# First unit of attention: v sent from its own tile to the tiles the products read, asked for one step later

## The chip, the cores and the metric

The kernel runs on one core of one Trainium2 chip. The metric is the device time of one execution in microseconds (us); of several runs the median counts. The engines of the core work side by side, each through its own instructions in order: TensorE (PE, with its weight loads PEld), VectorE (DVE), ScalarE (ACT), GpSimd (POOL), and SyncE (SP), whose queue here issues every transfer between the core's on-chip memory and DRAM.

## What is computed

The input x has 2048 rows of 512. Six rows of modulation come from a small vector c. The kernel computes attention with 32 heads of width 16 and then a mixer with two further products and an MLP; the change lies in the attention alone:

```python
h = _layernorm(x, axis=-1) * (1 + ca) + sa
qkv = (h @ wqkv).reshape(B, S, 3, H, Dh).transpose(2, 0, 3, 1, 4)
q, k, v = qkv[0], qkv[1], qkv[2]
scores = jnp.einsum("bhqd,bhkd->bhqk", q, k) * (Dh ** -0.5)
p = _softmax(scores, axis=-1)
o = jnp.einsum("bhqk,bhkd->bhqd", p, v)
x = x + ga * (o.transpose(0, 2, 1, 3).reshape(B, S, D) @ wo)
h = _layernorm(x, axis=-1) * (1 + cb) + sb
x = x + gb * _B_ref(h, B_w1, B_w2, B_w3, B_w4)
```

## The kernel before

**Units and steps.** Attention is cut into 64 units: 4 chunks of 512 queries times 16 pairs of heads. A unit has 16 steps, one for each tile of 128 keys (kt 0 to 15), so there are 1024 steps s. In a step PE makes two score products (sc, L1001) and two score products of the step 24 ahead (mb, L985). DVE takes the maxima of the mb products (mx, L981), ACT the exponentials of the sc products (pt, L997), POOL the low half of the split probabilities (pt<-pt, L1049). Two blocks of three half steps later PE multiplies them by v (pv: L1075 for the high parts, four matmuls a step; L1072 for the low parts, four every two steps). The pv products of key tiles 4i to 4i+3 read v from the tile vst[i].

**Filler.** Between these blocks PE works off other products: those that make q, k and v (L338, L340, L342), those of the modulation rows (mr, L632), and later the mixer. A planner written into the kernel (class Sched) lays the order down when the program is built: it keeps a clock of its own for each engine and a credit for filler, and gives each block so much of it as the budget (800, 900, then 700 of its ns a step) allows. Where the attention needs something, drain or step pushes the generators on until the planner's flag is there, whatever the credit says.

**v.** The generator v_gen with v_tiles makes v in 16 tiles of 128 keys for 8 pairs of heads at once: twelve matmuls into one bank, then ACT (L752, L753), DVE (L738), ACT (L755) and POOL (L756) write the split parts into one of three rotating tiles vt. The function store, last in that chain, issues one transfer of 384 KB from vt to Vs in DRAM (Vs<-vt), in rows of 384 bytes. A tile vt can be written again by ACT when this transfer has read it. The attention reads Vs back by pair, four key tiles at a time (vst<-Vs, 192 KB, function load_v). For all units but the first these loads are issued by pv_part well ahead. For unit 0 the function before(s) does it: the table VAT names the steps before which the four groups are demanded, here -1, 1, 5 and 9; it drains until the planner takes the four stores of the group as landed, and then issues one load.

**Order on SP.** All transfers stand in one queue in the order in which the planner made them, and an instruction that waits there holds up those behind it. Between the v stores stand the rows of k and q for DRAM (Ks<-qk, Qs<-qk), the loads of the next units (qtl<-Qs, kst<-Ks), eight small writes of shifts for each unit (qtl<-nm), and the weights (wst).

Of the kernel before, what the change touches and what calls it, by code (L numbers as in the profile page):

```python
# [61 lines left out]
XL = 0  # L62
NQ = 6
NV = 3
VAT = (-1, 1, 5, 9)
NPT = 8
PLOAD = 3500.0
WLAT = 4000.0
# [228 lines left out]
def cA(n=CH):  # L297
    return n / 1.2 + 52


def cD(n=CH):
    return n / 0.96 + 69
# [7 lines left out]
def kernel(ctx, tc, A_x, A_wqkv, A_wo, B_w1, B_w2, B_w3, B_w4, c, w_mod, out):  # L310
    nc = tc.nc
    te, act, dve, pool, dma = nc.tensor, nc.scalar, nc.vector, nc.gpsimd, nc.sync
# [24 lines left out]
    def mm3(o, lh, ll, rh, rl, first, last):  # L337
        te.matmul(o, lh, rh, start=first, stop=False)  # L338
        yield
        te.matmul(o, lh, rl, start=False, stop=False)  # L340
        yield
        te.matmul(o, ll, rh, start=False, stop=last)  # L342
        yield

    def nsq(n):
        return 0.4405 * n + 6
# [9 lines left out]
    def v_hi(t):  # L356
        return t[:, :, 0:128].rearrange("p a (b n) -> p a b n", b=2)
# [20 lines left out]
    Vs = dr.tile([NP, P, NKT, 192], BF16, name="Vs")  # L378
# [13 lines left out]
    sch = Sched()  # L392
    done = set()
    psd = {"s": False}

    def dbank(n):
        return sch.take(lambda i: psd["d"].tile([P, CH], F32, name=n, tag=("v" if i == NSM else f"s{i}") if psd["s"] else f"d{i}", bufs=1))
# [58 lines left out]
    def halves(w, nk):  # L456

        return [w[:, i].rearrange("p (k n) -> p k n", k=nk) for i in range(2)]
# [256 lines left out]
        done.add(("v", a))  # L715

    vlive, vrs = [], [0]

    def v_tiles(w, a, kts):
        wh, wl = halves(w, KT)  # L720
        for kt in kts:
            ci, t = divmod(kt, TPC)
            h = hT[ci]
            yield lambda: len(vlive) < NV and vrs[0] < 2 and sch.room() and ("hT", ci) in done
            vrs[0] += 1
            vlive.append(kt)
            b = dbank("v")[:, :256]
            for k in range(KT):
                for _ in mm3(b, h[:, k, 0, t * P:(t + 1) * P], h[:, k, 1, t * P:(t + 1) * P],
                             wh[:, k], wl[:, k], k == 0, k == KT - 1):  # L730
                    yield nsq(256)
            w = vt[kt % NV]
            v, vl = v_hi(w), v_lo(w)
            b3 = b.rearrange("p (a b d) -> p a b d", b=2, d=DH)
            r = qp.tile([P, H // 4, 2, DH], F32, name="vr", tag="vr", bufs=2)

            def rest(v=v, b3=b3, r=r, b=b):
                dve.tensor_tensor(r, b3, v[:, :, :, 0:DH], op=OP.subtract)  # L738
                sch.free(b)

            def store(kt=kt, w=w):
                vrs[0] -= 1

                def gone():
                    vlive.remove(kt)
                    if kt % 4 == 3:
                        done.add(("v", a, kt // 4))
                e = sch.dma(dma.dma_start, Vs[8 * a:8 * a + 8, :, kt, :].rearrange("a p n -> p a n"),
                            w)
                sch.after(e, gone)  # L750

            sch.chain(("A", cA(256), lambda v=v, b3=b3: act.activation(v[:, :, :, 0:DH], b3, AF.Copy)),  # L752
                      ("A", cA(256), lambda vl=vl, b3=b3: act.activation(vl[:, :, :, 8:8 + DH], b3, AF.Copy, scale=1.0 / VHI)),  # L753
                      ("D", cD(256), rest),
                      ("A", cA(256), lambda v=v, r=r: act.activation(v[:, :, :, VD:VD + DH], r, AF.Copy)),  # L755
                      ("G", cG(256), lambda v=v, r=r: pool.tensor_tensor(v[:, :, :, 2 * VD:2 * VD + DH], r, v[:, :, :, VD:VD + DH],  # L756
                                                                         op=OP.subtract)),
                      (None, 0, store), prio=VP, bank=b)
# [130 lines left out]
    def drain(flag):  # L889
        while flag not in done:  # L890
            sch.step()
# [45 lines left out]
    unit_tiles(at, 1, pool, pool)  # L937
    qst, mxs, osb = {}, {}, {}
    vst = [at.tile([P, NKT // 4, 192], BF16, name=f"vst{i}") for i in range(4)]
    pv, pt = {}, {}  # L940
    pts = [at.tile([P, 2, CH], I32, name=f"pt{i}") for i in range(NPT)]

# [11 lines left out]
    def load_v(u, i):  # L954

        if (u, i) in vnext or not u:
            vnext.discard((u, i))
            if u:
                drain(("v", units[u][1] // 8, i))
            sch.dma(dma.dma_start, vst[i], Vs[units[u][1], :, 4 * i:4 * i + 4])  # L960
# [585 lines left out]
    def before(s):  # L1546

        if s > NS // NC and s % (NS // NC) == 16:
            drain(("oT", s // (NS // NC) - 1))
        nu, r = divmod(s + 32, 16)  # L1550
        if r == 0 and 0 < nu < NU:
            ci, pr = units[nu]
            drain(("kq", pr // 4))
            if ci:
                drain(("q", pr // 8))
            load_unit(nu)
        if s in VAT:
            drain(("v", 0, VAT.index(s)))
            load_v(0, VAT.index(s))
        if s == NS - 12:  # L1560
            done.add("keys")
        if s == -12:
            unit_tiles(at, 2, dve, pool)
# [109 lines left out]
```

## Time and profile before

| | us |
|---|---|
| median of 3 runs | 2008.15 (2007.61 to 2010.73) |
| the profiled execution | 2010.86 |
| its span | 2009.1 |
| PE busy in the span | 1920.7 (96%) |
| POOL busy | 1678.7 (84%) |
| DVE busy | 1652.4 (82%) |
| ACT busy | 1467.5 (73%) |

The profiled execution took 2010.86 us, of which the span of the records is 2009.1. Start of unit 0 (its first sc product) is at 97.66 us of the span. The profile puts every wait down to what came last, by engine and line; the time an engine sat idle stands in brackets with it. A row of the timeline has the start, the time until the last of a merged group ended, the engine and line, the names (out<-in) and the count. The granted clock of TensorE is given as a share of its 2.4 GHz.

### The profile page before, as it was taken

Reading aid. Unit: us, or ns where it says so; the run is one execution under the profiler, and the core shown is the slowest. Engines: PE = TensorE matmul, PEld = TensorE weight load, DVE = VectorE, ACT = ScalarE, POOL = GpSimd, SP = SyncE. Lnnn points to the kernel's source line nnn. Section 1 sums busy time; section 2 is a strip of 40 time slices with the busy share of each in tenths; the row PEclk is TensorE's granted clock in tenths of the full one; section 3 lists DMA queues with packets and bytes.
Section 4 is the critical chain, followed back from the end, with each engine's and each line's share of the span. In section 5 each row is a group of like instructions: output and inputs, shape, how many; then the busy total and the mean of one; then the engine's idle time right before and its main releaser. Section 6 shows DMA issues by size and latency. Waiting matters only on the chain.

```text
span 2009.1 us, 42336 instructions
## 1 busy us (share of the span) xinstructions
PE 1920.7 (96%) x14464; PEld 1143.8 (57%) x14464; DVE 1652.4 (82%) x3025; ACT 1467.5 (73%) x3074; POOL 1678.7 (84%) x1611
## 2 busy tenths in 40 slices
PE   6899999999899999999999999999999999999899
PEld 4655554555454555555455555555545555555798
DVE  8878888788998988888989888898898889892643
ACT  5365889778878887777878777787787778786443
POOL 5376999899999998888999998898898989897532
PEclk8999999999999999999999999999999999999999
DMA  5764777876553334344433333344433343333432
GB/s 187 203 193 148 209 226 229 263 233 200 190 172 110 114 111 149 94 136 160 125 114 98 108 108 112 110 135 136 152 102 98 112 134 116 110 116 111 182 143 90
DMA packets 230624, 293.24 MB, mean 146 GB/s; under 512 B 123636, under 2 KB 175348, under 8 KB 214120
## 3 DMA queue, kind: packets, MB, share of 16 engines
q1 hardware_dynamic: 230408, 290.53, 46.2%
q8 instruction: 115, 1.88, 0.4%
q14 instruction: 101, 0.83, 0.1%
HBM read 226.49 MB, written 62.91 MB: 144 GB/s over the span
## 4 chain that ended last, share of the span: by engine, by line
PE 65%; DVE 17%; ACT 8%; POOL 3%; issue 3%; DMA 2%; SPq 1%; POOLq 0%; ACTq 0%; DVEq 0%
PE mb L985 13%; DVE mx L981 10%; PE sc L1001 10%; PE pv L1075 10%; PE w L338 7%; PE w L342 6%; PE w L340 6%; PE pv L1072 4%; ACT pt L997 4%; POOL pt L1049 2%; PE mr L632 1%; DVE xs L1400 1%; DVE sq L1397 1%; ACT pt L126 1%; PE ot L1104 1%
## 5 line engine op out<-in xcount | busy, mean ns | idle before, releaser
L1049 POOL TENSOR_SCALAR pt<-pt 128x1024 f16<-128x1024 uint16 x992 | 1317.2, 1364 | 129.2 <-ACT pt L997 123.8
L981 DVE TENSOR_REDUCE mx<-mb 128x1 f32<-128x512 f32 x2048 | 1278.7, 680 | 77.5 <-PE mb L985 52.0
L997 ACT ACTIVATE pt<-sc 128x512 int32<-128x512 f32 x2048 | 1088.3, 608 | 273.9 <-PE mb L985 212.0
L985 PE MATMUL mb<-kst,qtl 64*128 64x512 f32 x2048 | 750.5, 453 | 46.8 <-ACT pt L997 14.3
L1001 PE MATMUL sc<-qtl,kst 64*128 64x512 f32 x2048 | 720.1, 445 | 5.2 <-DVE mx L981 1.9
L985 PEld LDWEIGHTS mb<-kst,qtl 64*128 64x128 f32 x2048 | 347.9, 193 | 248.7 <-DVE mx L981 90.1
L1001 PEld LDWEIGHTS sc<-qtl,kst 64*128 64x128 f32 x2048 | 337.1, 186 | 160.3 <-DVE mx L981 53.4
L1075 PE MATMUL pv<-pt,vst 128*32 128x512 f16 x4096 | 359.8, 398 | 3.5 <-DMA vst<-Vs 3.5
L1072 PE MATMUL pv<-pt,vst 128*25 128x512 f16 (+1 forms) x2048 | 211.7, 395 | 2.0 <-POOL pt L1049 1.9
L1075 PEld LDWEIGHTS <-vst 128*32 128x32 bf16 x4096 | 91.2, 95 | 170.6 <-issue 109.5
L338 PE MATMUL w<-A,wr 128*128 128x256 f32 (+2 forms) x576 | 175.6, 305 | 1.0 <-ACT A L332 0.6
L1407 POOL TENSOR_TENSOR g<-xs,g 128x256 fp32r<-128x256 f32 (+2 forms) x144 | 102.9, 716 | 86.9 <-ACT g L1406 84.7
L340 PE MATMUL w<-A,wr 128*128 128x256 f32 (+2 forms) x576 | 170.1, 295 | 0.7 <-DVE A L328 0.7
L342 PE MATMUL w<-A,wr 128*128 128x256 f32 (+2 forms) x576 | 167.5, 291 | 0.0
L338 PEld LDWEIGHTS w<-A,wr 128*128 128x128 f32 x576 | 109.7, 190 | 36.1 <-ACT pt L997 13.2
L338 PE MATMUL w<-wr,g 128*128 128x512 f32 x288 | 119.3, 414 | 0.6 <-ACT g L1406 0.6
L340 PEld LDWEIGHTS w<-A,wr 128*128 128x128 f32 x576 | 109.9, 191 | 13.2 <-issue 12.0
L342 PE MATMUL w<-wr,g 128*128 128x512 f32 x288 | 115.0, 399 | 0.7 <-POOL g L1407 0.7
L1514 DVE TENSOR_TENSOR x<-x,w 128x512 f32<-128x512 f32 x64 | 43.9, 686 | 85.5 <-PE w L342 85.4
L340 PE MATMUL w<-wr,g 128*128 128x512 f32 x288 | 113.7, 395 | 0.0
L342 PEld LDWEIGHTS w<-A,wr 128*128 128x128 f32 x576 | 110.0, 191 | 5.6 <-issue 5.6
L1403 ACT ACTIVATE sq<-w 128x256 f32<-128x256 f32 (+2 forms) x144 | 55.8, 387 | 72.3 <-PE w L342 69.6
(147 smaller groups left out, 2079.5 us busy)
## 6 DMA issues: line engine op xcount, KB each, us to landing
wr<-Ws SPq DMA_DIRECT2D x80, 1024.0 KB
vst<-Vs SPq DMA_DIRECT2D x256, 192.0 KB
kst<-Ks SPq DMA_DIRECT2D x189, 256.0 KB
qtl<-Qs SPq DMA_DIRECT2D x192, 64.0 KB
Vs<-vt SPq DMA_DIRECT2D x32, 384.0 KB
Ws<-wq SPq DMA_DIRECT2D x40, 256.0 KB
Ws<-wst SPq DMA_DIRECT2D x40, 256.0 KB
wst<-in_B_w_dram SPq DMA_DIRECT2D x36, 256.0 KB
```

What stands on the lines that cost most here:

```text
L338: te.matmul(o, lh, rh, start=first, stop=False)
L340: te.matmul(o, lh, rl, start=False, stop=False)
L342: te.matmul(o, ll, rh, start=False, stop=last)
L981: end = sch.crit("D", 605, e + PX, lambda: dve.reduce_max(mxs[u][:, j, g, c:c + 1], b, axis=AX.X))
L985: return ready, lambda: te.matmul(b, lhs, kst[u % 3][r, c * CH:(c + 1) * CH], start=True, stop=True), after
L997: ea = sch.crit("A", 480, e + PX, lambda: act.activation(pt[s][:, j], b, AF.Exp))
L1001: return ready, lambda: te.matmul(b, kst[u % 3][r, kt * P:(kt + 1) * P], qst[u][r], start=True, stop=True), after
L1049: e_low[s] = XP["G"] + sch.crit("G", 1345, ready, lambda: pool.tensor_scalar(o, i, 0.5, 1.0, op0=OP.mult, op1=OP.mult))
L1072: te.matmul(acc[r:r + n, :], v[:, (kt + i) % 4, c - n:c].bitcast(F16), pt[s + i].bitcast(F16)[:, j, 0::2], start=False, stop=kt == NKT - 2 ...
L1075: te.matmul(acc[r:r + 32, :], v[:, kt % 4, r:r + 32], pt[s].bitcast(F16)[:, j, 1::2], start=kt == 0, stop=False, skip_group_check=True)
L1403: sch.chain(("A", cA(n), lambda: act.activation(sq, b, AF.Square)), ("D", cD(n), cube), ("A", cA(n), lambda: act.activation(sq, sq, AF.Tan ...
L1407: ("G", cG(n), lambda: pool.tensor_tensor(lo, xs, hi, op=OP.subtract)), (None, 0, end), bank=b)
```

## The change

Unit 0 no longer reads its v back from DRAM where that can be avoided. For each tile of the first v pass (a = 0) that is stored after the attention's tiles exist, store issues one more transfer, ahead of the one to Vs: the part of pair 0, 128 rows of 384 bytes, from vt straight into its place in vst. That holds for key tiles 2 to 15, fourteen transfers of 48 KB. Key tiles 0 and 1 were stored before and are loaded from Vs one at a time (2 transfers of 48 KB). The four loads of 192 KB fall away. The demands move from steps -1, 1, 5, 9 to -1, 2, 6, 10, and what they wait for is now, in the planner, that store has been issued, not that it has landed.

```diff
-VAT = (-1, 1, 5, 9)
+VAT = (-1, 2, 6, 10)
...
+    direct, near = [], set()
...
             def store(kt=kt, w=w):
                 vrs[0] -= 1
 
+                if not a and direct:
+                    sch.dma(dma.dma_start, direct[kt // 4][:, kt % 4], w[:, 0])
+                    near.add(kt)
+
                 def gone():
                     vlive.remove(kt)
+                    done.add(("vk", a, kt))
                     if kt % 4 == 3:
                         done.add(("v", a, kt // 4))
...
     vst = [at.tile([P, NKT // 4, 192], BF16, name=f"vst{i}") for i in range(4)]
+    direct += vst
...
         if s in VAT:
-            drain(("v", 0, VAT.index(s)))
-            load_v(0, VAT.index(s))
+            i = VAT.index(s)
+            for kt in range(4 * i, 4 * i + 4):
+                while kt not in near and ("vk", 0, kt) not in done:
+                    sch.step()
+                if kt not in near:
+                    sch.dma(dma.dma_start, vst[i][:, kt % 4], Vs[0, :, kt])
```

Because the planner sees other drains and other times on SP, it lays the filler down otherwise. On PE the order differs between the first v products beside attention and step 231; before it and from step 232 on, the matmuls stand in the same order in both. Up to step 0 and up to step 9 as much filler has been done in both. From there 24 matmuls of k that stood between steps 24 and 30 come later, so that from step 30 on the filler is behind by up to 29 matmuls' worth of 512 columns (26 at step 30, 21 at step 40, 19 at step 104); the arrears are made up between steps 112 and 136, and after a small lead both are level at step 232.

SP, from the load or copy that fills vst for key tile 12 on; vst_607 is the tile vst[3], vst_604 is vst[0], which here is filled for unit 1. The kernel before:

```order
L105 DMA qtl_600<-nm 1x128x2 x8
L105 DMA vst_604<-Vs 128x768
L105 DMA Vs<-vt_172 128x8x192
L105 DMA Vs<-vt_164 128x8x192
L105 DMA Qs<-qk_158 128x2x512
L105 DMA Qs<-qk_159 128x512
L105 DMA wst_118<-in_A_wqkv_dram 128x2x128 x2
L105 DMA wst_114<-in_A_wqkv_dram 128x2x128 x2
L105 DMA vst_607<-Vs 128x768
```

The changed kernel:

```order
L105 DMA vst_607<-vt_164 128x192
L105 DMA Vs<-vt_164 128x8x192
L105 DMA qtl_600<-nm 1x128x2 x8
L105 DMA vst_604<-Vs 128x768
L105 DMA vst_607<-vt_168 128x192
L105 DMA Vs<-vt_168 128x8x192
L105 DMA vst_607<-vt_172 128x192
L105 DMA Vs<-vt_172 128x8x192
L105 DMA Qs<-qk_158 128x2x512
L105 DMA Qs<-qk_159 128x512
L105 DMA vst_607<-vt_164 128x192
L105 DMA Vs<-vt_164 128x8x192
```

The one load of vst[3], which stood behind the last stores, the q rows and four weight loads, is replaced by four copies, the first of them ahead of the eight small writes; key tile 13 is stored behind those writes instead of ahead of them, and key tile 15 behind the q rows.

POOL at the same place (pt_615 is the low half of step 7, nm the shifts of a unit). The kernel before:

```order
L756 TENSOR_TENSOR vt_168<-vr,vt_168 128x8x2x16
L1034 TENSOR_TENSOR nm<-mf,nm 128x8
L756 TENSOR_TENSOR vt_172<-vr,vt_172 128x8x2x16
L756 TENSOR_TENSOR vt_164<-vr,vt_164 128x8x2x16
L1049 TENSOR_SCALAR pt_615<-pt_615 128x1024
L1049 TENSOR_SCALAR pt_608<-pt_608 128x1024
```

The changed kernel:

```order
L762 TENSOR_TENSOR vt_164<-vr,vt_164 128x8x2x16
L1041 TENSOR_TENSOR nm<-mf,nm 128x8
L762 TENSOR_TENSOR vt_168<-vr,vt_168 128x8x2x16
L762 TENSOR_TENSOR vt_172<-vr,vt_172 128x8x2x16
L762 TENSOR_TENSOR vt_164<-vr,vt_164 128x8x2x16
L1056 TENSOR_SCALAR pt_615<-pt_615 128x1024
L1056 TENSOR_SCALAR pt_608<-pt_608 128x1024
```

Three tiles of v instead of two stand directly ahead of the low half of step 7; behind them 18 low halves follow in a row, where it were 16.

ACT some steps later (wp is a split of weights that waits for a weight load). The kernel before:

```order
L997 ACTIVATE pt_614<-sc 128x512 x2
L440 ACTIVATE wp<-wst_118 128x512
L997 ACTIVATE pt_615<-sc 128x512 x2
L440 ACTIVATE wp<-wst_114 128x512
L997 ACTIVATE pt_608<-sc 128x512 x2
L997 ACTIVATE pt_609<-sc 128x512 x2
L997 ACTIVATE pt_610<-sc 128x512 x2
L1093 ACTIVATE ac<-pv 128x512
```

The changed kernel:

```order
L1004 ACTIVATE pt_610<-sc 128x512 x2
L1100 ACTIVATE ac<-pv 128x512
L1004 ACTIVATE pt_611<-sc 128x512 x2
L1004 ACTIVATE pt_612<-sc 128x512 x2
L1004 ACTIVATE pt_613<-sc 128x512 x2
L1004 ACTIVATE pt_614<-sc 128x512 x2
L1004 ACTIVATE pt_615<-sc 128x512 x2
L1004 ACTIVATE pt_608<-sc 128x512 x2
L440 ACTIVATE wp<-wst_114 128x512
L440 ACTIVATE wp<-wst_115 128x512
```

The two weight splits, which stood among the last exponentials of unit 0, now come six steps into unit 1's products, behind the copy ac of unit 0's result.

## Rows read from the trace of the kernel before

**Rows 1.** The page: span, busy time of each engine, granted clock in 40 slices.

```profile
span 2009.1 us, 42336 instructions
PE 1920.7 (96%) x14464; PEld 1143.8 (57%) x14464; DVE 1652.4 (82%) x3025; ACT 1467.5 (73%) x3074; POOL 1678.7 (84%) x1611
PEclk8999999999999999999999999999999999999999
```

**Rows 2.** Waits from 60 to 200 us: total, times, longest.

```profile
POOL pt L1049 <- ACT pt L997: 25.9, 21, 4.5
...
PE pv L1075 <- DMA vst<-Vs: 3.5, 1, 3.5
```

**Rows 3.** Timeline of PE around that wait.

```profile
128.33 0.40 PE L1072 MATMUL pv<-pt,vst 128*17 128x512 f16 x4
132.25 0.62 PE L1075 MATMUL pv<-pt,vst 128*32 128x512 f16 x4 [3.52 <-DMA vst<-Vs]
```

**Rows 4.** Engines by stretch: busy us (count), then PEclk, DMA share, GB/s.

```profile
120.00:128.60 8.60, 8.38 (x76) 3.66 (x72) 8.29 (x14) 6.48 (x13) 8.60 (x7) 1.00 0.79 213
132.30:139.00 6.70, 6.70 (x38) 3.90 (x42) 5.08 (x8) 3.29 (x7) 3.47 (x3) 0.52 0.76 222
316.00:345.00 29.00, 27.94 (x207) 14.58 (x205) 24.51 (x43) 26.96 (x58) 28.84 (x27) 1.00 0.75 225
```

**Rows 5.** Timeline of SP, 110 to 130 us.

```profile
114.53 0.36 SPq L105 DMA_DIRECT2D Vs<-vt  x1
116.08 5.22 SPq L105 DMA_DIRECT2D qtl<-nm  x8
121.35 0.59 SPq L105 DMA_DIRECT2D vst<-Vs  x1
122.04 1.00 SPq L105 DMA_DIRECT2D Vs<-vt  x2
123.14 2.21 SPq L105 DMA_DIRECT2D Qs<-qk  x2
125.39 3.48 SPq L105 DMA_DIRECT2D wst<-in_A_wqkv_dram  x4
128.97 0.41 SPq L105 DMA_DIRECT2D vst<-Vs  x1
```

**Rows 6.** Timeline of POOL, 119 to 150 us.

```profile
119.82 10.34 POOL L1049 TENSOR_SCALAR pt<-pt 128x1024 f16<-128x1024 uint16 x8
132.08 1.34 POOL L1049 TENSOR_SCALAR pt<-pt 128x1024 f16<-128x1024 uint16 x1 [1.91 <-ACT pt L997]
134.92 1.33 POOL L1049 TENSOR_SCALAR pt<-pt 128x1024 f16<-128x1024 uint16 x1 [1.50 <-ACT pt L997]
137.99 2.65 POOL L1049 TENSOR_SCALAR pt<-pt 128x1024 f16<-128x1024 uint16 x2 [1.73 <-ACT pt L997]
141.40 5.21 POOL L1049 TENSOR_SCALAR pt<-pt 128x1024 f16<-128x1024 uint16 x4 [0.76 <-ACT pt L997]
146.89 2.69 POOL L1049 TENSOR_SCALAR pt<-pt 128x1024 f16<-128x1024 uint16 x2
```

**Rows 7.** Timeline of ACT: the last tile of v, and the weight split.

```profile
117.47 0.36 ACT L752 ACTIVATE vt<-v 128x256 bf16<-128x256 f32 x1
118.66 0.42 ACT L755 ACTIVATE vt<-vr 128x256 bf16<-128x256 f32 x1 [0.55 <-DVE vr L738]
...
130.32 0.63 ACT L440 ACTIVATE wp<-wst 128x512 fp32r<-128x512 f32 x1 [2.45 <-DMA wst<-in_A_wqkv_dram]
```

**Rows 8.** A store's landing: its issue on SP, and ACT's wait for it.

```profile
66.66 3.52 SPq L105 DMA_DIRECT2D Vs<-vt  x3
...
71.09 0.39 ACT L752 ACTIVATE vt<-v 128x256 bf16<-128x256 f32 x1 [1.56 <-DMA Vs<-vt]
```

**Rows 9.** Waits of SP from 60 to 130 us.

```profile
SPq L105 <- POOL vt L756: 11.1, 6, 3.5
SPq L105 <- DMA Vs<-vt: 2.6, 1, 2.6
```

**Rows 10.** PE: products of filler in a row (k of 512 columns, v of 256).

```profile
105.30 0.40 PE L340 MATMUL k<-hT,wp 128*128 128x512 f32 x1
105.53 0.39 PE L342 MATMUL k<-hT,wp 128*128 128x512 f32 x1
...
116.45 0.28 PE L340 MATMUL v<-wp,hT 128*128 128x256 f32 x1
116.57 0.28 PE L342 MATMUL v<-wp,hT 128*128 128x256 f32 x1
```

## The prediction

> **What bounds the kernel now.** I read the page first. PE is busy for 1920.7 of 2009.1 us and its granted clock is almost everywhere full [rows 1], so over the whole span PE sets the time, with POOL, DVE and ACT behind it. But the change reaches only unit 0 and, by the planner, the filler up to step 231; what follows has the same matmul order. So I read that stretch alone. The waits of the stretch show one in which PE waits for a transfer: 3.5 us, once, for vst<-Vs [rows 2]. The timeline of PE places it at 128.7 to 132.25 us, before a product of the high parts [rows 3]. The timeline of SP says why. The load that releases it is issued at 128.97 and lands at 132.25, 3.3 us later; it was issued so late because it stands behind the last two stores of v, two transfers of q and four weight loads, and waited 2.6 us for the last store to land [rows 5, 9]. The load brings all of key tiles 12 to 15, and PE wanted tile 12, which had been ready for long.
>
> A second row belongs to it. From 132.3 to 139.0 us the granted clock is 0.52 of full, that is almost throughout at the lower level of 1.2 GHz, directly behind the wait, and PE is busy all through [rows 4]. Third, the stretch around it has hardly any filler. There the engines of the softmax decide: POOL is busy 8.60 of 8.60 us up to the wait, and then 3.47 of 6.70 [rows 4]. Its timeline has eight low halves in 10.34 us, 1.30 each, then gaps of 1.91, 1.50, 1.73 and 0.76 us behind ACT [rows 6]. In that stretch ACT also waits 2.45 us for a weight load [rows 7].
>
> **The change part by part.** *The load of tiles 12 to 15 goes.* Tile 12 is now copied by a transfer that stands ahead of the eight small writes and not behind everything else. The store of the tile there was issued at 114.53 [rows 5]; a copy in its place is due some 13 us before the product at 128.7. The copies of tiles 13 to 15 come behind the small writes and the refill of vst[0], from 121.4 on, and then behind the q rows, about 125.6. A store of 384 KB landed 71.09 - 66.66 = 4.4 us after its issue [rows 8]; a copy is an eighth of that with rows of the same 384 bytes, so it lands within 0 to 4.4 us, and I take the 3.3 us of the load that PE waited for. Tile 15 is then there at 129. Its product is due three steps after tile 12's, at 128.7 + 3 x 1.30 = 132.6. The wait of 3.5 us goes.
>
> *The low clock.* It cost 6.70 x (1 - 0.52) = 3.2 us of PE's full speed [rows 4]. It followed the wait, so it may go too. The bounds are 0 and 3.2; together with the wait 3.5 to 6.7 us.
>
> *What is late next.* Both amounts are PE time, and PE is not all that counts here: the low halves on POOL go at 1.30 us a step. In the change POOL does three tiles of v and then the low halves of steps 7 to 24 in a row. When does that row begin? Up to step 9 PE has as much filler as before, only the last tile of v now stands behind q, so it ends where q ended, at about 119.4. Before, the last tile took from ACT's first copy at 117.47 to POOL's end at 119.82, 2.4 us [rows 6, 7]; now that runs from 119.4 to 121.8. Then 18 x 1.30 = 23.4 us give 145.2. Before, step 24 ended at 146.89 + 2.69 = 149.6 [rows 6]. The gain at step 24 is 4.4 us. The weight splits that held ACT for 2.45 us stand behind step 24 in the change, and their loads are issued some ten steps ahead, so I cost them at nothing; if the cover is gone it is those 2.45 us again.
>
> *The filler that comes later.* At step 24 three k matmuls are owed, at 0.23 us each [rows 10] 0.7 us, which the 4.4 us contain: 3.7 remain. From steps 24 to 40 the arrears grow to 21 matmuls, 4.9 us; PE does so much less there, and that is no gain, since it must be paid. It is paid from step 112 to 136. Were that stretch POOL's alone, all of it would be free; POOL is busy 28.84 of 29.00 us there, but PE 27.94 too [rows 4]. So the bounds are 0 and 4.9 us of further gain; the row leaves 1.1 us of PE, and I take that.
>
> *SP.* Fourteen copies are added, two small loads take the place of four larger ones. At 0.36 us an issue [rows 5] fourteen cost 5.0 us, at the 0.65 of the small writes (5.22 / 8) 9.1, spread over 60 to 126 us. In that time SP waits 11.1 us for POOL's tiles of v alone [rows 9], and that wait hides them. Uncovered, each copy delays the release of a tile vt, since its store is issued behind it. For the last tile it matters: it reuses the buffer of tile 12, whose store leaves at about 115.0 and by [rows 8] lands at 119.4, just when ACT wants to write. No slack, but no cost that I can see.
>
> Sum: 3.7 + 1.1 = 4.8 us. The profiled execution goes from 2010.86 to 2006.1, and the median, 2.7 us below it, from 2008.15 to **2003.3 us**.
>
> **The rivals.** *All of it counts.* POOL may catch up while PE works off other filler, so that PE's 6.7 us come through, and half of the arrears are hidden (2.5 us): 9.2 us, 1999.0. For it speaks that PE is the busiest engine over the span; against it POOL's 8.60 of 8.60.
>
> *The low clock comes again.* The change has a stretch without filler from step 9 to about 29, longer than before, in which PE waits for POOL's row. The lower level came here behind a wait of PE. A stretch like that of [rows 4] costs 3.2 us again: gain 1.6, 2006.5. Against it speaks the stretch up to 128.6, also without filler, at clock 1.00.
>
> *The copies don't do it.* Suppose each copy is served only when the one ahead of it has landed, at 4.4 us each [rows 8]. Three from 121.4 on land at 134.6, 2.0 us past the product at 132.6; the stores between them could make it 3.6. Gain 4.8 - 3.6 = 1.2, 2007.0. Against it: SP issued two stores in 1.00 us [rows 5], without waiting for the first. The Trainium skill, DMA: Bandwidth & Descriptors, speaks against small copies: its Specifications want 512 bytes or more for full rate and name a read-modify-write below that, and the copies have rows of 384. Its section on the anatomy of one DMA gives about 2.0 us fixed plus the bytes at 436 GB/s, so 2.1 us a copy as an estimate; three one after another would land at 127.7, early enough. No row of the trace has such a copy alone, and the stores of 384-byte rows agree with no more than that small rows are slow.
>
> *Slower: ACT is held by the last tile.* ACT works in order. If it waits for the buffer of tile 12, the exponentials from step 9 on stand behind it, and with them POOL and PE. Every us past 119.4 then costs one. It decides against the change when it takes more than 4.8 us, and measurably from 8.8, a landing after 128.2. In the load's case a store and the wait together took from 122.04 to 128.97 [rows 5], 6.9 us. Twice that, 13.8 from 115.0, is 128.8: 9.4 us lost against 4.8 gained, 2012.7. The stores between 60 and 119 us show only 1.6 us of such a wait at most [rows 8], so this is unlikely.
>
> **How the numbers follow.** Forecast 0.44, all of it 0.17, low clock again 0.22, copies late 0.10, ACT held 0.07. A measurement of this kernel can tell about 0.2% from no change, 4.0 us: faster means below 2004.1, slower above 2012.2. Of the forecast's 0.44 some 0.07 lies above 2004.1 (arrears paid in full give 2004.4), which leaves 0.37; with the 0.17 and 0.02 of the low clock at a smaller price that is 0.56 for faster. Same has 0.07 + 0.20 + 0.10 = 0.37, slower 0.07. The range goes from 1998.5, just below the case where all counts, to 2008.5, past the late copies; it leaves out the slower case, some 0.05 of still larger gains, up to 11.6 us with all arrears hidden, and 0.04 of late copies at a higher price.
>
> **What would show it.** After: no wait of PE for vst in unit 0; the copies in vst issued from about 115 us on; POOL's low halves of steps 7 to 24 without gaps, step 24 done near 145; no half clock around 132; the first k products of unit 1's time not before POOL's row ends. It is wrong if PE waits for vst again, if ACT's last tile of v waits for a store by more than 1 us, or if step 24 is earlier but step 232 is not: then the arrears took it.

## The result, and the profile after

| | before | after |
|---|---|---|
| median, us (10 runs each) | 2009.71 (2007.47 to 2014.79) | 2014.48 (2008.31 to 2020.71) |
| the profiled execution | 2010.86 | 2010.97 |
| its span | 2009.1 | 2009.2 |

The change makes the kernel slower: the ratio is 1.0028, interval 1.0016 to 1.0041. The forecast was 2003.3, range 1998.5 to 2008.5: a gain of 4.8 us, where 4.8 us were lost. The two profiled executions are level; the one of after is among the shorter of its ten. On the page of the changed kernel (span, busy time, granted clock by slices; compare [rows 1]) PE and DVE are as busy as before. POOL is 8.5 us busier and ACT 5.7 us less busy: between units 3 and 13 the planner now gives POOL five low halves (pt<-pt) that ACT did before, in two instructions each:

```profile
span 2009.2 us, 42358 instructions
PE 1920.1 (96%) x14464; PEld 1145.6 (57%) x14464; DVE 1651.0 (82%) x3025; ACT 1461.8 (73%) x3064; POOL 1687.2 (84%) x1616
...
PEclk8999999899999999999999999999999999999999
```

What the prediction said of unit 0 came out almost to the microsecond. PE's timeline after, at the products that read vst[3] (compare [rows 3]), has no wait for v:

```profile
128.83 0.63 PE L1082 MATMUL pv<-pt,vst 128*32 128x512 f16 x8
129.29 0.39 PE L1079 MATMUL pv<-pt,vst 128*17 128x512 f16 x4
129.52 0.40 PE L1082 MATMUL pv<-pt,vst 128*32 128x512 f16 x4
```

POOL's low halves of steps 7 to 24 run in one row (compare [rows 6]), from 122.37 to 145.6, where 121.8 to 145.2 was forecast; before they ended at 149.6:

```profile
122.37 23.22 POOL L1056 TENSOR_SCALAR pt<-pt 128x1024 f16<-128x1024 uint16 x18
```

The copies of tiles 12 to 15 stand on SP's timeline where the order said (compare [rows 5]); each holds SP for 0.5 to 1.2 us. The trace also records when a transfer's completion reached its semaphore, which no view prints: these four landed 4.3, 2.2, 2.8 and 3.4 us after their issue, the fourteen of them 1.8 to 4.3 us after it. The prediction took 3.3 within 0 to 4.4.

```profile
113.37 0.96 SPq L105 DMA_DIRECT2D vst<-vt  x1
...
121.47 0.49 SPq L105 DMA_DIRECT2D vst<-vt  x1
...
122.69 0.54 SPq L105 DMA_DIRECT2D vst<-vt  x1
...
126.08 1.18 SPq L105 DMA_DIRECT2D vst<-vt  x1
```

The half clock at 132 us is gone (by stretch: engines' busy us, then PEclk, DMA share, GB/s; in [rows 4] the clock was 0.52):

```profile
132.30:139.00 6.70, 6.46 (x64) 3.47 (x64) 5.51 (x11) 4.80 (x10) 6.70 (x6) 1.00 0.79 231
```

A unit ends with ACT's copy ac of its result, and these copies are the milestones from here on. ACT's timeline of before, units 0, 7 and 9 (the first unit is 0):

```profile
139.67 0.60 ACT L1093 ACTIVATE ac<-pv 128x512 f32<-128x512 f32 x1 [0.85 <-PE pv L1072]
...
332.27 0.78 ACT L1093 ACTIVATE ac<-pv 128x512 f32<-128x512 f32 x1
...
392.87 0.63 ACT L1093 ACTIVATE ac<-pv 128x512 f32<-128x512 f32 x1
```

And of after:

```profile
134.51 0.60 ACT L1100 ACTIVATE ac<-pv 128x512 f32<-128x512 f32 x1 [1.02 <-PE pv L1079]
...
329.40 0.63 ACT L1100 ACTIVATE ac<-pv 128x512 f32<-128x512 f32 x1
...
398.08 0.62 ACT L1100 ACTIVATE ac<-pv 128x512 f32<-128x512 f32 x1
```

Unit 0 ends 5.2 us earlier, unit 7 only 2.9 us earlier, and unit 9 5.2 us later. So 2.3 us are given back over seven units, and 8.1 us are lost within two. Those two hold something that before does not have: two waits of ACT, and behind each one of PE. ACT's timeline after:

```profile
335.48 0.72 ACT L888 ACTIVATE wq<-wst 128x512 fp32r<-128x512 f32 x1
...
336.45 0.61 ACT L888 ACTIVATE wq<-wst 128x512 fp32r<-128x512 f32 x1
...
339.80 0.64 ACT L888 ACTIVATE wq<-wst 128x512 fp32r<-128x512 f32 x1
...
347.82 0.63 ACT L888 ACTIVATE wq<-wst 128x512 fp32r<-128x512 f32 x1 [2.88 <-DMA Ws<-wq]
...
388.91 0.63 ACT L888 ACTIVATE wq<-wst 128x512 fp32r<-128x512 f32 x1 [3.49 <-POOL wst L875]
```

PE's timeline after, at the same places:

```profile
348.99 0.50 PE L992 MATMUL mb<-kst,qtl 64*128 64x512 f32 x1 [2.55 <-ACT pt L1004]
...
390.07 0.98 PE L1008 MATMUL sc<-qtl,kst 64*128 64x512 f32 x2 [2.41 <-ACT pt L1004]
```

L888 is part of the filler that prepares the weights of the later products: ACT writes the high part of a piece of weights to one of three rotating tiles wq, POOL or DVE the low part, and both go to DRAM (Ws). The changed order puts three such pieces close together, at 335 to 340 us; the fourth needs the first one's buffer back. Two timelines say why it is not back in time. POOL's has its low part done at 338.60:

```profile
337.31 1.29 POOL L890 TENSOR_TENSOR wst<-wst,wq 128x512 fp32r<-128x512 f32 x1
```

SP's has its store behind the eight small writes of the next unit's shifts and two loads; it leaves at 343.57, five us after it could have:

```profile
336.57 5.81 SPq L105 DMA_DIRECT2D qtl<-nm  x8
...
343.57 0.43 SPq L105 DMA_DIRECT2D Ws<-wq  x1
```

The second wait is for POOL, which multiplies a piece by its row (L875) only after three low halves of the softmax and the low part of another piece (L890, ended at 387.66). In the kernel before ACT does one low half for POOL there, at 378.72. POOL's timeline after:

```profile
382.50 3.95 POOL L1056 TENSOR_SCALAR pt<-pt 128x1024 f16<-128x1024 uint16 x3
386.36 1.30 POOL L890 TENSOR_TENSOR wst<-wst,wq 128x512 fp32r<-128x512 f32 x1
387.60 1.27 POOL L875 TENSOR_TENSOR wst<-wst,sbrow 128x512 f32<-128x512 f32 x1
```

ACT works in order, so the exponentials stand behind both waits, and PE behind those. The stretches of the two waits, of before:

```profile
346.00:363.00 17.00, 16.08 (x114) 7.46 (x106) 14.85 (x22) 12.78 (x26) 14.81 (x12) 0.90 0.69 210
...
380.00:398.00 18.00, 16.55 (x98) 10.10 (x96) 11.34 (x19) 12.96 (x26) 13.42 (x11) 1.00 0.98 310
```

And of after:

```profile
346.00:363.00 17.00, 14.45 (x78) 7.31 (x70) 10.61 (x16) 9.17 (x18) 10.48 (x9) 0.70 0.96 324
...
380.00:398.00 18.00, 15.59 (x94) 8.19 (x93) 11.84 (x17) 10.20 (x20) 15.20 (x12) 0.91 0.90 292
```

PE is busy 2.6 us less in the two together, and its granted clock is 0.70 instead of 0.90 in the first and 0.91 instead of 1.00 in the second: about 1 us behind the end of each wait it falls to the lower level for a while. The two waits of PE are 5.0 us, and the lower clock takes up to 0.20 x 17 + 0.09 x 18 = 5.0 us of full speed more, which together is enough for the 8.1 us lost. Filler is no part of it: counted in products of 512 columns, after is level with before at the end of unit 7 and 3 ahead at the end of unit 9. The Trainium skill, TensorE: Matmul & The Clock Gate, describes how the clock falls and rises again where TensorE waits for data over and over (its section on oscillation). The trace agrees in that a wait of PE stood before each of the two falls; both are single waits of 2.4 to 2.6 us, and no run shows here what a wait needs to bring the clock down.

After unit 9 the profiled execution of after wins the 5.2 us back until unit 31 (990.86 and 990.66), for the most part in steps that fall on stretches of half clock that before has there and after has not. That is luck of this one execution: the second trace of after (run 3) is still 2.7 us behind there, and the other executions left no trace.

### The profile page after: what moved, and what is told of

Same layout as the page of the kernel before. It is cut to its first block, busy times and chain, and to the rows that moved or that the text cites. A ratio compares the mean times of both kernels' runs of the same rounds, so it can differ in the third digit from the quotient of the medians.

```text
span 2009.2 us, 42358 instructions
## 1 busy us (share of the span) xinstructions
PE 1920.1 (96%) x14464; PEld 1145.6 (57%) x14464; DVE 1651.0 (82%) x3025; ACT 1461.8 (73%) x3064; POOL 1687.2 (84%) x1616
## 4 chain that ended last, share of the span: by engine, by line
PE 66%; DVE 17%; ACT 8%; POOL 3%; issue 3%; DMA 2%; SPq 1%; POOLq 0%; ACTq 0%; DVEq 0%
PE mb L992 14%; DVE mx L988 10%; PE sc L1008 10%; PE pv L1082 10%; PE w L338 7%; PE w L340 6%; PE w L342 6%; PE pv L1079 4%; ACT pt L1004 4%; POOL pt L1056 2%; DVE xs L1407 1%; PE ot L1111 1%; DVE sq L1404 1%; SPq L105 1%; PE mr L632 1%
```

## The experiments

A difference of 0.2% is near what the half clock does by itself from one execution to the next. So a second figure stands beside each ratio: an execution whose mean granted clock is c spends about (1 - c) x 2 of its span at half clock, and over some 200 executions of all these kernels one us of half clock went with 0.28 us of time within a kernel. With each kernel's mean brought to 55 us of half clock by that, **before** gives 2009.5, 2009.3 and 2009.6 in the three sets that the experiments below were timed in (runs 1 to 4; 5 to 8; 9 to 11), **after** 2013.8 (error 0.5). The figure takes out part of what a wait costs when the half clock follows it, so it is an aid and not a verdict.

**1. The copies in the order of before.** PE, VectorE, ACT and POOL do the work of before in its own order; only SP gets the fourteen copies in the place of the loads.

```diff
...
+                if not a and direct:
+                    dma.dma_start(direct[kt // 4][:, kt % 4], w[:, 0])
+                    near.add(kt)
...
-            load_v(0, VAT.index(s))
+            i = VAT.index(s)
+            for kt in range(4 * i, 4 * i + 4):
+                if kt not in near:
+                    dma.dma_start(vst[i][:, kt % 4], Vs[0, :, kt])
+            sch.dma(lambda o, x: None, vst[i], Vs[0, :, 4 * i:4 * i + 4])
```

> The copies of the change, with the order of the kernel before on PE, DVE, ACT and POOL word for word: the planner doesn't count the copies, and the demands stay at steps -1, 1, 5, 9. Theory O (the new order of the filler costs more than the copies give): the 3.5 us wait goes and nothing else changes, so 3 to 6 us under the kernel before, ratio 0.997 to 0.9985, no PE wait for vst, unit 0 done some 4 us earlier and the lead kept to the end. Theory T (the fourteen copies on SP and the late release of vt cost more than the wait): slower than the kernel before by 3 to 6 us, as the change is.

Measured: 2011.94 against 2009.24, ratio 1.0013 (0.9999 to 1.0028); at equal half clock 2010.0. PE's wait for v is gone, and unit 0 ends where it did, 139.66 against 139.67. ACT's timeline of this kernel:

```profile
132.65 0.63 ACT L440 ACTIVATE wp<-wst 128x512 fp32r<-128x512 f32 x1 [3.73 <-DMA wst<-in_A_wqkv_dram]
...
139.66 0.60 ACT L1099 ACTIVATE ac<-pv 128x512 f32<-128x512 f32 x1 [0.39 <-PE pv L1078]
```

PE's, 1.2 us on:

```profile
133.82 0.50 PE L1007 MATMUL sc<-qtl,kst 64*128 64x512 f32 x1 [3.14 <-ACT pt L1003]
```

The wait for weights that [rows 7] shows at 2.45 us lay beside the wait for v all along. It grows to 3.73, because the copies push the weight loads back on SP (the first of the four is issued at 128.19 instead of 125.39 [rows 5]), and it takes the place of the one removed. Neither expectation came: no gain of 3 to 6 us, and no such loss.

**2. The order of after with the loads of before.** The four engines do the work of after, word for word (with POOL's five low halves more), and v comes by the four loads at the new steps.

```diff
-                    sch.dma(dma.dma_start, direct[kt // 4][:, kt % 4], w[:, 0])
+                    sch.dma(lambda o, x: None, direct[kt // 4][:, kt % 4], w[:, 0])
...
-                    sch.dma(dma.dma_start, vst[i][:, kt % 4], Vs[0, :, kt])
+                    sch.dma(lambda o, x: None, vst[i][:, kt % 4], Vs[0, :, kt])
+            dma.dma_start(vst[i], Vs[0, :, 4 * i:4 * i + 4])
```

> The order of the changed kernel on PE, DVE, ACT and POOL word for word, but v for unit 0 comes by the four old loads from DRAM, issued at the new steps -1, 2, 6, 10. Theory O: the wait of PE for vst is back and adds to the loss, 3 to 7 us above the changed kernel, ratio to before 1.004 to 1.007. Theory T: without the copies the loss is gone, within 2 us of the kernel before.

Measured: 2016.42, ratio 1.0044 (1.0026 to 1.0063); at equal half clock 2015.6 (error 0.9). PE waits for v again, but for less than before:

```profile
132.04 0.62 PE L1082 MATMUL pv<-pt,vst 128*32 128x512 f16 x4 [2.23 <-DMA vst<-Vs]
```

ACT's timeline of the same kernel, the end of unit 0 and the wait of unit 8:

```profile
137.03 0.60 ACT L1100 ACTIVATE ac<-pv 128x512 f32<-128x512 f32 x1 [0.41 <-PE pv L1079]
...
350.38 0.63 ACT L888 ACTIVATE wq<-wst 128x512 fp32r<-128x512 f32 x1 [2.34 <-DMA Ws<-wq]
```

Half of unit 0's gain (2.6 of 5.2 us) is thus the order's and not the copies', and the loss between units 7 and 9 is here without any copy (unit 9 ends 5.3 us later than before). The order alone, with the five low halves that it moves to POOL, makes the kernel slower; order and low halves weren't tried apart. That the wait for v would come on top of the changed kernel's loss was a miss: run 3, timed beside it, took longer.

**3. The changed kernel again**, beside runs 1, 2 and 4 on the same chip.

> The changed kernel once more, for a second trace and times beside the others. Theory O: ratio to before 1.002 to 1.004 again; where its time is above the first trace's, the trace shows more stretches at half clock in steps 24 to 232. Theory T: the same ratio, with the additional time in the waits of SP and ACT between 60 and 130 us.

Measured: 2021.22, ratio 1.0055 (1.0034 to 1.0077). Unit 0 ends 3.9 us earlier, unit 7 0.9 earlier, unit 9 4.3 later. ACT waits again at the same pieces:

```profile
349.36 0.63 ACT L888 ACTIVATE wq<-wst 128x512 fp32r<-128x512 f32 x1 [2.46 <-DMA Ws<-wq]
```

The second wait is there too, with 3.50 us. So the mechanism repeats, and the loss is at least that of the first comparison. Why it is about twice as large this time (at equal half clock 2017.8, error 1.4) isn't settled; the expectation was 1.002 to 1.004.

**4. The later steps alone.** In the kernel before only the table changes.

```diff
-VAT = (-1, 1, 5, 9)
+VAT = (-1, 2, 6, 10)
```

> The kernel before with nothing but the demands at steps -1, 2, 6, 10, old loads. It has a third order of the filler. Theory O: another order, another result, anywhere within 6 us of before, with the wait of PE for vst of 3 us or more, since the load comes later. Theory T: as before or slower by the longer wait, 0 to 4 us.

Measured: 2020.37, ratio 1.0058 (1.0036 to 1.0080), from four runs. It gives a third order, with unit 0 1.5 us later and unit 9 13.9 us later, some of which comes back. It doesn't tell what the later step does in the changed kernel: there the copies with the old steps -1, 1, 5, 9 give the same program on all engines as with the new ones, so that the step changes nothing. What it shows is how much an order can cost: 11 us, where at most 6 were expected.

**5. The copies in the order of before, and the two pieces of weights early.** As run 1, and the loads for the splits that ACT waited for are issued behind the store of key tile 12.

```diff
...
+                if not a and kt == EARLY:
+                    for i in range(2):
+                        early[2, i] = t = wst[i]
+                        f3 = t.bitcast(F32).rearrange("p (k n) -> p k n", n=2 * P)
+                        for m in range(2):
+                            dma.dma_start(f3[:, :, m * P:(m + 1) * P], kpn(A_wqkv[i * 2 * P:(i + 1) * 2 * P, m * D + 2 * P:m * D + 3 * P]))
...
-            e = sch.dma(dma.dma_start, f3[:, :, o:o + x.shape[2]], x)
+            e = sch.dma((lambda o, i: None) if key in early else dma.dma_start, f3[:, :, o:o + x.shape[2]], x)
```

> Old order on PE, DVE, ACT and POOL with the copies, as in c_old_order_copies, and the four weight loads for which ACT waited 3.73 us there are issued ahead of the small writes of the shifts (behind the store of key tile 12) and not behind the q rows. Theory O2 (two waits lay side by side in unit 0, PE's for vst and ACT's for these weights, and taking one leaves the other): both are gone, unit 0 ends 3 to 5 us earlier than in the kernel before, the lead stays, ratio 0.997 to 0.9985. Rival R (the stretch is bound by POOL's and DVE's work, so no wait there counts): unit 0 ends less than 1 us earlier, ratio 0.9995 to 1.0015.

Measured: 2006.65 against 2007.45, ratio 0.9994 (0.9983 to 1.0004); at equal half clock 2007.6 (error 0.5). ACT's wait is gone, and unit 0 still ends at 139.36, so the 3 to 5 us expected there did not come. By that number the rival (POOL and DVE bind the stretch) would fit as well; runs 10 and 11 settle it. PE's timeline shows a third wait that lay under the other two:

```profile
134.58 2.05 PE L637 MATMUL mr<-wst,sil 128*128 128x128 f32 x8 [3.58 <-DMA wst<-in_w_mod_dram]
```

It is for a piece of the modulation's weights, whose load is late on SP for the same reason, since it stands behind the q rows:

```profile
128.56 1.21 SPq L106 DMA_DIRECT2D wst<-in_w_mod_dram  x1
```

**6. The changed kernel with ACT's two waits taken away.** The store of the one piece whose buffer came back late no longer reads that buffer, so that it needn't be waited for (this kernel leaves out that piece's high part in DRAM; the low part stands there twice); the row product of the fourth piece of wo goes to VectorE instead of POOL.

```diff
...
-                ops.append(("G", cG(), lambda f=f, r=rows[nm]: pool.tensor_tensor(f, f, r, op=OP.mult)))
+                ops.append(("G", cG(), lambda f=f, r=rows[nm], eng=dve if (nm, k) == ("wo", 3) else pool: eng.tensor_tensor(f, f, r, op=OP.mult)))
...
-                for h, t in enumerate((w.bitcast(F32), f)):
+                for h, t in enumerate((f if num == 14 else w.bitcast(F32), f)):
```

> The changed kernel without the two waits of ACT at 347.8 (2.88 us, for the store of a weight piece) and 388.9 us (3.49 us, for POOL's product of a weight piece): the store of that one piece's high half reads another tile (its high half in DRAM is then wrong, its low half twice there), and the one product runs on DVE instead of POOL. Theory O: these waits stopped PE for 2.5 and 2.4 us and took its clock down behind each, so 4 to 8 us come back by unit 9, ratio to before 0.9995 to 1.001. Rival S (the loss after unit 7 is the work that had been put off, not the waits): under 2 us come back, ratio 1.002 to 1.005.

Measured: 2012.76, ratio 1.0022 (1.0008 to 1.0035); at equal half clock 2011.4 (error 0.6). That is 2.1 above before, where after was 4.3 above it in the first comparison and 8.3 in run 3. Unit 9 ends 1.1 us later than before instead of 5.2; counted from the end of unit 7, this kernel loses 0.9 us to before, and after 8.1. The two stretches of this kernel:

```profile
346.00:363.00 17.00, 15.33 (x106) 7.69 (x106) 12.03 (x18) 10.41 (x20) 14.20 (x12) 0.90 0.95 321
...
380.00:398.00 18.00, 17.60 (x109) 9.32 (x109) 14.26 (x22) 13.86 (x27) 17.13 (x14) 1.00 0.95 299
```

PE's clock is back at before's 0.90 and 1.00, and PE is busy 2.9 us more than in after. The two waits, with the half clock behind them, are thus the cause of the loss between units 7 and 9. They aren't all that the kernel lost: the ratio's interval still lies above 1. Where the remaining 2 us go isn't settled. In the profiled execution of this kernel the lead is gone by unit 7 already; its one large item there is a wait of PE for DVE, 5.29 us to 153.00, with half clock around it, at a place where after waits too, for 1.48 us (shown further down). This execution ran with more half clock than that of any other kernel, and can't say what the others lost.

**7 and 8. Other orders without any copy.** The kernel before with one number of the planner other: its assumed latency of a transfer, 2300 instead of 2200 ns, or that of a weight load, 4100 instead of 4000. Each lays the filler out anew, the first over steps 0 to 240, the second from step 65 on.

```diff
-DBW, DLAT = 360.0, 2200.0
+DBW, DLAT = 360.0, 2300.0
```

```diff
-WLAT = 4000.0
+WLAT = 4100.0
```

> The kernel before with one number of the planner changed: it takes a transfer to land 2300 instead of 2200 of its ns after its issue. The same work and the same loads, another order of the filler from step 0 to 240. Theory O (before's order is the best of many tried, and any other order of the filler costs some us by chance waits): slower than before by 2 to 8 us, ratio 1.001 to 1.004. Rival S: the change's loss is due to what it put off, so this one is within 2 us of before.

> The kernel before with another number of the planner changed: weight loads are taken to need 4100 instead of 4000 of its ns. Another order of the filler from step 65 to 240 only; unit 0 is untouched. Theory O: slower than before by 1 to 7 us, ratio 1.0005 to 1.0035, with units 0 to 3 ending as in before. Rival S: within 2 us of before.

Measured: 2011.38, ratio 1.0022 (1.0011 to 1.0033), and 2009.19, ratio 1.0005 (0.9994 to 1.0016). The first number, which has no meaning for the work at all, costs about as much (4 us) as the forecast said that the change would gain; the second costs nothing that can be told.

**9. The changed kernel in another order.** Copies and steps as in the change, with the 2300 of run 7.

> The changed kernel with one number of the planner other (its assumed latency of a transfer 2300 instead of 2200), which lays the filler out anew over steps 0 to 247; copies and demanded steps are those of the change. Theory (what the change lost, it lost to the order that the planner happened to lay): the first unit ends 3 us or more earlier than before as in the changed kernel, and the waits of ACT near 348 and 389 us are not those of the changed kernel; the time lies anywhere from 0.998 to 1.005, and if it is under 1.0010 the loss is that of one order and not of the copies. Rival (the copies or the later step cost the loss in any order): ratio 1.002 to 1.005 with the first unit still early and the loss again between units 7 and 9.

Measured: 2008.65 against 2007.58, ratio 1.0003 (0.9992 to 1.0013); at equal half clock 2010.7 (error 0.4), 1 us above before. Unit 0 ends 1.5 us earlier than before and unit 9 4.1 us earlier. The two stretches:

```profile
346.00:363.00 17.00, 15.81 (x124) 7.71 (x116) 15.24 (x25) 12.57 (x26) 13.89 (x12) 1.00 0.93 294
...
380.00:398.00 18.00, 17.36 (x113) 9.28 (x111) 14.32 (x24) 15.62 (x31) 15.96 (x14) 1.00 0.92 309
```

No half clock, no wait of ACT for a piece of weights but one of 0.45 us, and PE busy 3.1 us more than in after. The copies are the same, so the loss belongs to the one order that the planner happened to lay for them. Two of the conditions held (no such loss, a time under 1.0010); that unit 0 ends only 1.5 us earlier and not 3 was a miss.

**10 and 11. All three weight transfers early, in the order of before: with the copies, and without them.** As run 5, and the piece of the modulation's weights is issued early too. The second kernel has no copies and loads v as before; the engines do the same work in the same order in both, and as in before.

```diff
...
+                if not a and kt == EARLY:
+                    early["m", 2, 0] = t = wst[2]
+                    dma.dma_start(t.bitcast(F32).rearrange("p (k n) -> p k n", n=P), kpn(w_mod[:, 2 * D:2 * D + P]))
+                    for i in range(2):
+                        early[2, i] = t = wst[i]
...
```

> TensorE, VectorE, ScalarE and GpSimd do the work of the kernel before in its own order; new are the copies of v (issued by the store of each v tile, not counted by the planner, demanded at -1, 1, 5, 9), and three weight transfers for the staging tiles of the next projection weights (the two wst pieces that ACT splits and the one piece of w_mod that TensorE waited for) are issued behind the store of key tile 12 instead of some 20 us later. Theory of the side-by-side waits: with all three gone TensorE has nothing left to wait for there; the first unit ends 3 to 5 us earlier than before (139.7), the half clock at 132 goes, and since the order is the old one nothing new stands at units 7 to 9: ratio 0.9970 to 0.9985, some 3 to 6 us under the kernel before. Rival (POOL's row of low halves sets the unit's end whatever TensorE waits for): the first unit ends within 0.5 us of before, ratio 0.9990 to 1.0005.

> The same with the four old loads of v from DRAM at their old steps instead of the copies: it leaves the change out and keeps only the three early weight transfers. Theory: TensorE's wait for vst stays (about 3.5 us at 132) and covers the other waits; the first unit ends within 0.5 us of before, ratio 0.9990 to 1.0005; together with the run before it, this says what the copies alone are worth once nothing else waits there. Rival (the weight transfers were the cause, and v's load only stood behind them in SP's queue): the wait for vst shrinks to under 1.5 us and the first unit ends 2 us or more earlier, without any copy.

Measured, against 2007.58: with the copies 2005.64, ratio 0.9985 (0.9974 to 0.9996); without them 2004.18, ratio 0.9981 (0.9972 to 0.9990). At equal half clock 2007.8 (error 0.5) and 2006.9 (error 0.4). With the copies, ACT's timeline has the end of unit 0 at

```profile
134.66 0.60 ACT L1112 ACTIVATE ac<-pv 128x512 f32<-128x512 f32 x1 [0.62 <-PE pv L1091]
```

and without them at

```profile
134.28 0.60 ACT L1107 ACTIVATE ac<-pv 128x512 f32<-128x512 f32 x1 [0.17 <-PE pv L1086]
```

Both are 5 us earlier than before, and both stay 5 to 6 us ahead through units 7 to 9. The wait for v, which no copy removes in the second kernel, shrinks by itself (PE's timeline):

```profile
129.63 0.41 PE L1089 MATMUL pv<-pt,vst 128*32 128x512 f16 x4 [0.93 <-DMA vst<-Vs]
```

SP's timeline of that kernel shows how. The four weight transfers leave at 108.43, and the load of v is issued at 126.92 instead of 128.97 [rows 5]:

```profile
108.43 2.07 SPq L756 DMA_DIRECT2D wst<-in_A_wqkv_dram  x4
...
126.92 0.33 SPq L106 DMA_DIRECT2D vst<-Vs  x1
```

The rival of the second expectation is right: the weight transfers were the cause, and v's load only stood behind them. My theory there, a wait of 3.5 us that stays, fell. Once they are out of the way the copies bring nothing more. The kernel without them beats both the kernel before and the changed one:

```profile
span 1998.3 us, 42340 instructions
PE 1912.5 (96%) x14464; PEld 1141.5 (57%) x14464; DVE 1653.0 (83%) x3025; ACT 1467.3 (73%) x3074; POOL 1680.0 (84%) x1611
```

## Why the prediction was wrong, step by step

**The wait for v, the half clock, POOL's row: the size was right, the cause only half.** Step 24 was to be done 4.4 us earlier; POOL's row ended 4.0 us earlier, and unit 0 ended 5.2 us earlier. But the prediction gave this to the copies. Run 1 shows that the copies alone move the end of unit 0 by nothing, since ACT's wait for weights stands beside the one for v, and run 5 that one more stands under both. The prediction had that row [rows 7] and the condition, "if the cover is gone it is those 2.45 us again". What it missed is that all three loads are late for one reason, the queue on SP around 125 us, and that their waits run at the same time, so that the last one left sets the end. It also read one row wrongly: the 2.6 us that SP waited for a store [rows 9] ended at 111.83, before the load of tiles 8 to 11; the load at 128.97 followed the weight loads without a wait. In after the gain came through because the new order moved ACT's splits away: run 2 has half of it without a copy.

**"The filler that comes later", and the weight splits "at nothing".** 1.1 us of the 4.9 us of arrears were to be hidden when they are paid, so that 4.8 us would remain once the filler is level again. That much was right in kind: at the end of unit 6 after is 19.5 products of 512 columns behind, at the end of unit 7 it is level; at 0.23 us each [rows 10] these are 4.5 us, and after falls back by 2.8, from 5.7 to 2.9 us ahead, so that 1.7 us were hidden. What didn't last was the rest of the sum, the lead without what was owed: 4.7 us at the end of unit 0, 2.3 at the end of unit 4 (6.0 ahead, 16 products or 3.7 us behind), 1.2 at the end of unit 6. So 2.9 us were left at unit 7 in the first profile of after, and 0.9 in the second. A part of it is the weight splits, which the change moves behind step 24 and the prediction cost at nothing. DVE does their low parts among its maxima (its timeline after, then PE's):

```profile
147.79 1.78 DVE L438 TENSOR_TENSOR wp<-wst,wp 128x512 fp32r<-128x512 f32 x1
...
150.83 0.50 PE L992 MATMUL mb<-kst,qtl 64*128 64x512 f32 x1 [1.48 <-DVE mx L988]
```

Behind that wait the clock falls. The stretch of after (in before it is at 1.00 there):

```profile
152.00:156.00 4.00, 4.00 (x26) 2.62 (x19) 2.45 (x4) 1.09 (x2) 3.72 (x4) 0.57 0.78 234
```

That is 1.7 us of full speed. The same wait, of 1.1 us or more, with half clock beside it stands in all five traces of the change's order and run 9's. In the five with the order of before there is none; two of these have such a stretch of half clock later, at 173 to 180 us. The rest isn't settled.

**"What follows has the same matmul order", and the stretch up to step 231: the step that failed.** The prediction treated the new order as a matter of when filler is paid, and priced it from one stretch, 316 to 345 us [rows 4]; its sum, 3.7 + 1.1 us, has no term for what the order does to ACT, POOL and SP. The damage, 8.1 us between the ends of units 7 and 9, lies right behind that stretch. It isn't PE's filler but ACT's and POOL's pieces of weights, which the planner lays among the exponentials by its own clock; three close together and eight small writes on SP cost ACT 2.9 us, a POOL that is late costs it 3.5, PE waits 5.0 us behind the two, and half clock follows each. Run 2 shows the loss without copies, run 9 the copies without the loss, run 6 that without the two waits 0.9 us is lost there. The prediction used no row of ACT or SP beyond 150 us, and no order of theirs beyond unit 1. What the five low halves moved to POOL cost by themselves no run shows.

**The rivals.** "The low clock comes again" came true: the clock stayed at 1.00 in unit 0 and fell at 152 us, at the end of the stretch without filler that this rival named, for about half of its 3.2 us, though behind a wait for DVE and not for POOL. It fell again behind the new waits at 349 and 390 us, which no rival had. "The copies don't do it" is wrong as it was told: no product waited for a copy. The rule on rows under 512 bytes that stood beside it in the Trainium skill (DMA: Bandwidth & Descriptors, Specifications) did no visible harm: the copies landed 1.8 to 4.3 us after their issue, and those issued at 121.47 and 122.69 landed at 123.64 and 125.53 although a store of 384 KB stood between them. The 2.1 us of the prediction lie in that range, but the section behind them is about transfers that GpSimd issues, and these are SP's. "ACT is held by the last tile of v" didn't happen: ACT waited 0.8 us there, for PE. "All of it counts" fell. The result, slower, had a chance of 0.07, and that all on this one mechanism; no rival said that a re-laid order costs something elsewhere, though the front of the document lists an order that differs over more than 200 steps. Runs 4, 7 and 8 put that price between nothing and some 11 us.

**What would show it wrong.** The last sign named was "if step 24 is earlier but step 232 is not: then the arrears took it". The sign came; it was mostly not the arrears, which were paid by the end of unit 7 with 2.9 us still left.

**The profiled execution and the median.** The sum was made on the profiled pair and carried over to the median. The pair came out level, the medians 4.8 us apart: single executions of this kernel differ by more than the whole change, with the half clock that they happen to get.

## What to carry to other kernels

When a wait is to be removed, list every wait that ends within a few us of it on the other engines and look for what holds them all; here one in-order queue did, and moving three weight transfers forward in it was worth more than a new path for the data that was seen to be late. When a planner lays the work out anew, the change is the new order and not the lines of the diff: go through every engine's order to its last difference, and look for pieces that now stand closer together than their buffers come back. To know what an edit is worth by itself, run it once in the old order and run the new order once without it.

## What the runs showed of the hardware

A transfer of 1 KB holds SP about as long as a large one: the eight writes of a unit's shifts took 5.22 [rows 5] and, at 336.57 in after, 5.81 us together, 0.65 to 0.73 each, while the load of 192 KB of v took 0.41 [rows 5] and a copy of 48 KB 0.5 to 1.2. So eight small writes, with two loads behind them, could hold a store that was ready for five us, and with it ACT, PE and the clock.

The half clock differs between executions of one and the same kernel: of the ten runs of after the one with the lowest mean granted clock, 0.981, took 2020.71 us and the one with the highest, 0.990, took 2008.31. Differences of 0.2% here needed ten runs and more of each kernel, and an experiment in which only one thing differs.
